# Weight conversion: the sign comes from ScalarE's scaling step instead of a VectorE step

## The chip, the cores and the metric

One core of a Trainium2 chip. The metric is the device time of one execution in microseconds; the kernel before took 1156.26 us (median of 3 runs, 1155.57 to 1157.02).

## The reference

Three stages, computed in float32 on the chip. The weights `moe_*` and `moe2_*` come from numpy as 64-bit floats and are handed over as 64-bit words; q, k, v are 32-bit.

```python
q_n, k_n = rmsnorm(q, g_q), rmsnorm(k, g_k)          # 4 x 12 heads, 448 x 64
attn = softmax(q_n @ k_n.T / sqrt(64))
x = attn @ v                                         # -> 1792 x 768
x = ((x @ w1) * (x @ w2)) @ w3 @ w_out               # d_ff 1024
h = x @ w_in                                         # d_ff 2048
out = (h * clip(h + 3, 0, 6) / 6) @ w_out2
```

## The kernel before, in words

Attention runs over 24 pairs of heads in 192 steps (8 per pair) in a pipeline: in step t two matmuls give 112 x 448 scores (L631, L632), VectorE scales them and takes the maximum (L638, then L645), ScalarE takes the exponential one step later (L650), TensorE transposes (L657), ScalarE and VectorE evict (L666, L676), and the products with v follow (L709, L710). Every step then calls `fill(us, aux)`, which puts other work into the gaps: products of the first MLP (`filler`, so many microseconds of TensorE work per step), preparation of its weights (`prep`), and from the first batch of layer 2 on the conversion of weights for the second MLP (`early`).

The first MLP is reordered: `wprime` first multiplies w3 and w_out (matmuls at L256, from 9 to 197 us), then for each of 4 batches `layer1` (L395, L400) and `layer2` (L89 to L91). After 731 us only the second MLP is left (L1247, L1309), on weights that are 32-bit by then.

A weight tile of 64-bit floats is brought in by a DMA on SP's queue (`fetch`, tag `raw`, a ring of 4 slots of 128 x 384 or 128 x 512 double words; `wr`, 2 slots of 128 x 768, for the last eight tiles). `convert` makes 32-bit floats of it in four instructions. `hi` is the upper word of each number, `lo` the lower one, `top` the upper 16 bits of the lower word. L149 (ScalarE) reads `hi` as a 32-bit float and multiplies it by 2^-112, which moves the exponent to its new bias; L150 (ScalarE) turns `top` into the three low mantissa bits; L152 (VectorE) takes the sign bit out of `hi` and puts it into `lo`; L155 (VectorE) shifts `hi` left by three and joins `lo`. The shift pushes the sign bit of `hi` out at the top, which is why L152 saves it first.

The order around it is set by cost counters. Each `yield` of `convert` names a cost (0.7, 0.9, 0.9). `fill` gives `prep` a budget (`aux`: 3 per step while `wprime` runs, then 4 until 8 weights are used, then 2) and steps it until the budget is used up or until `reach` forbids the next item (tiles wait for buffers that products set free). `early` gets 0.95 per step, at most 1.9 saved up. In the prologue, before the first score, twelve items are run one by one by `unit`, with the loads, the norms and the first q and k written out by hand between them. From this program order the framework's scheduler makes the order on each engine by a simulated timeline; every engine, and SP's queue with the loads, then runs its instructions in that order, and each waits for its data.

Of the kernel before, what the change touches and what calls it, by code (L numbers as in the profile page):

```python
# [14 lines left out]
F32R = mybir.dt.float32r  # L15
I32 = mybir.dt.int32
U16 = mybir.dt.uint16
SIGN = -(1 << 31)
AF = mybir.ActivationFunctionType
ALU = mybir.AluOpType  # L20
AX = mybir.AxisListType
# [30 lines left out]
def fused_kernel(ctx: ExitStack, tc: tile.TileContext, nat, qT, kT, vin, gq, gk,  # L52
                 w12, w3t, wo, win, wo2, outT):
    nc = tc.nc
# [87 lines left out]
    def convert(w, r):  # L142

        hi, lo = r[:, :, 1], r[:, :, 0]
        top = r.bitcast(U16).rearrange("p n (t s) -> p n t s", s=2)[:, :, 0, 1]
        f = hi.bitcast(F32)
        nc.scalar.activation(f, f, AF.Copy, scale=2.0 ** -112)  # L149
        nc.scalar.activation(lo, top, AF.Copy, scale=2.0 ** -13, bias=2.0 ** -14 - 0.5)  # L150
        yield 0.7
        nc.vector.scalar_tensor_tensor(out=lo, in0=hi, scalar=SIGN, in1=lo,  # L152
                                       op0=ALU.bitwise_and, op1=ALU.bitwise_or)
        yield 0.9
        nc.vector.scalar_tensor_tensor(out=w, in0=hi, scalar=3, in1=lo,  # L155
                                       op0=ALU.logical_shift_left, op1=ALU.bitwise_or)
        yield 0.9


    prep = [None]  # L160
# [15 lines left out]
    def open_wprime():  # L176
# [29 lines left out]
        def item(q):  # L206
            kind, n, z = order[q]
            r = raw.pop(q)
            w = r.shape[1]
            if kind != "l":  # L210
                if kind == "c":
                    t = woh[n, z] = pool.tile([P, NH], F32, tag="woh", bufs=2 * M1, name="woh")
                else:
                    t = w3[n, z] = pool.tile([P, HF], F32, tag="w3", bufs=NA3, name="w3")
                if r.dtype == F32:
                    nc.gpsimd.tensor_copy(t, r)
                else:
                    yield from convert(t.bitcast(I32), r)
                load(q + 4)
                return  # L220
            if z == 0:
                W["first"][n] = W["hp"].tile([P, 2, DM], F32R, tag="ws", bufs=NF, name="ws")
            t = W["first"][n][:, :, z * NH : z * NH + NH]
            f = r
            if r.dtype != F32:
                wi = r[:, :, 0]
                yield from convert(wi, r)
                f = wi.bitcast(F32)
            nc.scalar.activation(t[:, 0, :], f, AF.Copy)
            yield w / 1200  # L230
            W["sub"] = nc.gpsimd.tensor_sub(t[:, 1, :], f, t[:, 0, :])
            if z == 1:
                dma(w12d[n // 2, 1 - n % 2], W["first"][n].bitcast(F32).rearrange("p t c -> p (t c)"))
            load(q + 4)
            yield 0.0
# [51 lines left out]
    def early():  # L287
        pool = L["xp"]
        todo = [(x, h) for x in reversed(EARLY) for h in range(2)]
        raws = []  # L290

        def load():
            if todo:
                (kind, q), h = todo.pop()
                cs = slice(h * NH, h * NH + NH)
                src = (win if kind == "in" else wo2)[q][:, cs]
                raws.append((fetch(pool, src, NH, "raw", 4), wfd[q + (M2 if kind == "out" else 0)][:, cs]))

        load()
        yield 0.5  # L300
        while raws:
            r, dst = raws.pop()
            load()
            w = pool.tile([P, NH, 2], I32, tag="raw", bufs=4, name="raw").rearrange("p n t -> p (n t)")[:, :NH]
            yield from convert(w, r)
            dma(dst, w.bitcast(F32))
            yield 0.0
# [133 lines left out]
    state = dict(debt=0.0, aux=0.0, early=0.0, spent=0.0, done=False)  # L441

    def fill(us, aux):

        state["aux"] = min(state["aux"] + aux, 2 * aux)
        while state["aux"] > 0 and prep[0] is not None:
            c = prep[0].step()
            if c is None:
                break
            state["aux"] -= c  # L450
        state["early"] = min(state["early"] + 0.95, 1.9)
        while state["early"] > 0 and "early" in L:
            c = next(L["early"], None)
            if c is None:
                break
            state["early"] -= c
        state["debt"] = min(state["debt"] + us, 2 * us)
        while state["debt"] > 0 and not state["done"]:
            try:
                c = next(filler)  # L460
            except StopIteration:
                state["done"] = True
                return
            if c is None:
                return
            state["debt"] -= c
            if "pool" in L:
                state["spent"] += c
# [5 lines left out]
    def attention(ap, rate):  # L474
# [273 lines left out]
        z = 4 * NC * D  # L748
# [4 lines left out]
            dma(T["nat", i], nat[i].rearrange("p a b d -> p (a b) d"))  # L753

        def unit(q, n):
            for z in range(4):
                prep[0].step()
            assert prep[0].done == q + 1
            load(n)

        load(0)
# [8 lines left out]
        dma(gs[:, 1:2], gk)  # L770
        nc.vector.tensor_mul(G, gs[:, 0:1], gs[:, 1:2])
        unit(0, 4)
        unit(1, 5)
        load_q(0)
        load_k(0)
# [7 lines left out]

        squares(0)
        unit(2, 6)
        squares(1)
        unit(3, 7)
# [36 lines left out]
        unit(11, 15)  # L824
        load_nat(4)
        fill(8.0, 0.0)
        queue[1] = False
        first = ExitStack()
# [51 lines left out]
        while t < 8 * NP + 23 or xs_ready:  # L880
            t += 1
            if t == 4:
                first.close()
            now[0] = t
            live = t < 8 * NP
            ps = score(*divmod(t, 8)) if live else None
            if 0 < t <= 8 * NP:
                expo(*divmod(t - 1, 8))
            u = t - LG
            if 0 <= u < 8 * NP and u % 8 < 7:  # L890
                trans(*divmod(u, 8))
            if 0 <= u - 1 < 8 * NP and (u - 1) % 8 < 7:
                tlo(*divmod(u - 1, 8))
            if live:
                scale_max(t // 8, t % 8, ps)
                negate(*divmod(t, 8))
            if 0 <= u < 8 * NP and u % 8 < 7:
                thi(*divmod(u, 8))
            if 0 <= u - 2 < 8 * NP and (u - 2) % 8 < 7:
                pv(*divmod(u - 2, 8))  # L900
            with ExitStack() as es:
                for a in anchors.get(t - (3 if "pool" in L else 2), ()):
                    es.enter_context(tc.issue_after(a.ins))
                fill(*rate(t))
            run_tasks()
            if "pool" in L:
                xnext()
# [254 lines left out]
    while not state["done"] or any(k >= now[0] for k in tasks):  # L1162
        now[0] += 1
        fill(2.0, 3.0)
        run_tasks()
        if "half" in L and xg is None:
            xo["cm"] = tc.tile_pool(name="xl", bufs=1, side="left", **RW)
            xo["pool", True] = d1.enter_context(xo["cm"])
            xg = xprep(0)
        with ExitStack() as es:  # L1170
            for z in L["gate"].values():
                es.enter_context(tc.issue_after(z.ins))
            if xg is None:
                spend(1.1)
            else:
                for _ in range(2):
                    if next(xg, None) is None:
                        prep_to(ready[0] + 1 if ready[0] < AHEAD2 else 0)
# [245 lines left out]
```

## Time and profile before

| | |
|---|---|
| median of 3 runs | 1156.26 us |
| profiled execution | 1154.9 us, span 1153.1 us |
| PE (matmul) busy | 1109.7 us, 96% |
| PEld (weight load) busy | 944.3 us, 82% |
| DVE (VectorE) busy | 924.0 us, 80%, 2047 instructions |
| ACT (ScalarE) busy | 815.5 us, 71%, 1729 instructions |
| POOL (GpSimd) busy | 185.9 us, 16% |
| DMA | 299.04 MB, 259 GB/s in the mean |

The profile is that of one execution. Busy shares are means over stages with different limits, so the stages have to be read one by one. L with a number is a line of the kernel; "x" a count of instructions; `raw<-raw` names the tile written and the tile read. The chain of waits follows the work that ended last back through whatever released it.

### The profile page before, as it was taken

The numbers are of one execution on the slowest core, as the hardware profiler recorded it, in microseconds if no ns is written. First come the engines' busy times: TensorE is split into PE (matmuls) and PEld (weight loads), VectorE is DVE, ScalarE is ACT, GpSimd is POOL, SyncE is SP. The second block draws the span as 40 slices with busy tenths as digits, with TensorE's granted clock in tenths as the row PEclk, the third lists the DMA queues.
The fourth block names the chain that finished last, engine by engine and source line by source line (L and its number), as shares of the span: only waits on it lengthen the run. The fifth ranks groups of instructions, "written<-read, shape, count | busy, mean of one in ns | idle before, by whom it ended". The sixth has DMA issues, their size and how long they took to land.

```text
span 1153.1 us, 17490 instructions
## 1 busy us (share of the span) xinstructions
PE 1109.7 (96%) x5483; PEld 944.3 (82%) x5483; DVE 924.0 (80%) x2047; ACT 815.5 (71%) x1729; POOL 185.9 (16%) x156
## 2 busy tenths in 40 slices
PE   5899899899999999999999999999999999999998
PEld 3455576788788888788999899899988989999897
DVE  7878988889878998889875345899988898887764
ACT  6888878888678877688675333766666776666664
POOL 1132422645422222223002000000000000000000
PEclk9999999999999999999999999999999999999999
DMA  8988845789999889898879989556469955435961
GB/s 266 332 269 292 268 156 155 232 271 292 329 314 326 287 307 310 275 306 278 274 268 313 393 327 349 218 199 208 163 224 381 368 169 169 154 109 174 343 233 73
DMA packets 109661, 299.04 MB, mean 259 GB/s; under 512 B 13280, under 2 KB 46048, under 8 KB 109568
## 3 DMA queue, kind: packets, MB, share of 16 engines
q1 hardware_dynamic: 109568, 297.93, 75.8%
q8 instruction: 43, 0.70, 0.3%
q14 instruction: 50, 0.41, 0.1%
HBM read 230.61 MB, written 67.27 MB: 258 GB/s over the span
## 4 chain that ended last, share of the span: by engine, by line
PE 59%; DVE 14%; DMA 12%; ACT 9%; issue 3%; SPq 1%; POOL 1%; ACTq 0%; POOLq 0%; DVEq 0%
PE acc L1309 17%; PE sB L1247 8%; PE sA L1247 8%; PE bank L395 6%; PE bank L256 4%; PE bank L400 3%; DVE PP L638 3%; PE bank L657 2%; DMA raw<-in_wo_dram 2%; DMA rsd<-rss 2%; DVE xl L676 2%; DMA rsb<-rsd 2%; DMA raw<-in_w_dram 2%; DVE raw L152 2%; DVE Q L604 2%
## 5 line engine op out<-in xcount | busy, mean ns | idle before, releaser
L1309 PE MATMUL acc<-g,wt 128*128 128x448 f32 x1008 | 214.8, 369 | 1.2 <-ACT g L1197 1.0
L1309 PEld LDWEIGHTS acc<-g,wt 128*128 128x128 f32 x1008 | 189.1, 188 | 20.6 <-ACT g L1197 1.9
L395 PE MATMUL bank<-xhl,ws 128*128 128x448 f32 x768 | 181.0, 367 | 2.8 <-ACT bs L416 1.5
L395 PEld LDWEIGHTS bank<-xhl,ws 128*128 128x128 f32 x768 | 143.6, 188 | 16.3 <-ACT bs L416 1.9
L650 ACT ACTIVATE PP<-PP,mx 112x448 f32<-112x448 f32 x192 | 127.3, 664 | 39.3 <-DVE mx L645 37.1
L638 DVE CUSTOM_DVE_ANT_0 PP<-bank,rb,rq 112x448 f32<-112x448 f32 x192 | 128.4, 673 | 12.3 <-PE bank L632 10.3
L256 PE MATMUL bank<-woh,w 128*128 128x384 f32 x256 | 99.9, 515 | 14.3 <-DVE woh L155 12.4
L1247 PE MATMUL sA<-xo,wt 128*128 128x448 f32 x504 | 112.0, 366 | 1.1 <-ACT u L1258 1.1
L1247 PE MATMUL sB<-xo,wt 128*128 128x448 f32 x504 | 112.2, 367 | 0.8 <-ACT u L1258 0.6
L1247 PEld LDWEIGHTS sB<-xo,wt 128*128 128x128 f32 x504 | 94.4, 188 | 9.9 <-ACT u L1258 1.9
L1247 PEld LDWEIGHTS sA<-xo,wt 128*128 128x128 f32 x504 | 94.6, 188 | 9.5 <-ACT u L1258 1.5
L657 PEld LDWEIGHTS bank<-ident,PP 112*128 112x128 f32 x672 | 77.8, 140 | 29.6 <-issue 8.8
L666 ACT ACTIVATE xh<-bank 128x448 fp32r<-128x448 f32 (+1 forms) x156 | 82.7, 538 | 27.3 <-PE bank L657 22.5
L152 DVE SCALAR_TENSOR_TENSOR raw<-raw 128x384 int32<-128x384 int32 (+1 forms) x112 | 69.3, 619 | 39.8 <-ACT raw L150 35.9
L676 DVE TENSOR_TENSOR xl<-bank,xh 128x448 fp32r<-128x448 f32 x142 | 86.8, 614 | 16.3 <-ACT xh L666 15.1
L657 PE MATMUL bank<-ident,PP 112*128 112x112 f32 x672 | 93.7, 260 | 4.7 <-DVE xl L676 3.0
L1016 DVE TENSOR_TENSOR wt<-wf,wt 128x384 fp32r<-128x384 f32 x160 | 86.8, 552 | 14.0 <-ACT wt L1015 13.8
L400 PE MATMUL bank<-xhl,ws 128*128 128x448 f32 x384 | 94.7, 366 | 0.0
L149 ACT ACTIVATE raw<-raw 128x384 f32<-128x384 f32 (+1 forms) x112 | 63.7, 569 | 41.4 <-DMA raw<-in_wo_dram 16.6
L631 PE MATMUL bank<-K,Q 128*112 128x448 f32 x192 | 79.9, 417 | 6.4 <-DVE mx L638 6.2
L256 PEld LDWEIGHTS bank<-woh,w 128*128 128x128 f32 x256 | 49.4, 199 | 43.8 <-DVE woh L155 15.5
L1015 ACT ACTIVATE wt<-wf 128x384 fp32r<-128x384 f32 x160 | 80.3, 517 | 2.9 <-PE acc L1309 2.7
(136 smaller groups left out, 2181.7 us busy)
## 6 DMA issues: line engine op xcount, KB each, us to landing
ws<-w12d SPq DMA_DIRECT2D x48, 768.0 KB
ws<-wpd SPq DMA_DIRECT2D x32, 768.0 KB
wf<-wfd SPq DMA_DIRECT2D x56, 384.0 KB
raw<-in_wo_dram SPq DMA_DIRECT2D x44, 384.0 KB
td<-G SPq DMA_DIRECT2D x32, 448.0 KB
G<-td SPq DMA_DIRECT2D x32, 448.0 KB
raw<-in_w_dram SPq DMA_DIRECT2D x32, 384.0 KB
w12d<-ws SPq DMA_DIRECT2D x16, 768.0 KB
```

Of the source, the lines that this page charges most:

```text
L152: nc.vector.scalar_tensor_tensor(out=lo, in0=hi, scalar=SIGN, in1=lo, op0=ALU.bitwise_and, op1=ALU.bitwise_or)
L256: nc.tensor.matmul(ps[:, :NH], W["w3"][a, c // 4][:, cs], W["woh"][c, n], start=c == 0, stop=c == M1 - 1)
L395: nc.tensor.matmul(ps[:, :S], w[:, 0, ks], x[:, y, :], start=k == 0 and y == 0, stop=False)
L400: nc.tensor.matmul(ps[:, :S], w[:, 1, ks], L["xhl"][i][:, 0, :], start=False, stop=k == KD - 1)
L638: anchors[8 * i + s].append(nc.vector.tensor_tensor_reduce(out=T["PP", i][:, c, sl], in0=ps[:CP, :S], in1=T["rb", i][:, sl], op0=ALU.mult, ...
L650: anchors[8 * i + s].append(nc.scalar.activation(v, v, AF.Exp, bias=T["m", i][:, 8 + s : 9 + s], accum_out=T["sum", i][:, s : s + 1]))
L657: nc.tensor.transpose(ps[:, c * CP : c * CP + CP], src[:, c, kb * P : kb * P + P], ident[:CP, :CP])
L666: nc.scalar.activation(hi, ps, AF.Copy)
L676: nc.vector.tensor_sub(lo, ps, hi)
L1016: nc.vector.tensor_sub(t[:, 1, :], src, t[:, 0, :])
L1247: mm = nc.tensor.matmul(ps[:, :S], w[:, a, ks], x[:, c, :], start=first and k == 0 and n == 0, stop=k == KD // 2 - 1 and n == 2, skip_grou ...
L1309: nc.tensor.matmul(ps, w[:, y, ns], x[:, z, :], start=first and a == 0, stop=end and a == 2, skip_group_check=h in "674")
```

## The change

ScalarE's scaling becomes a parametric rectifier: a value that is negative after the scale is also multiplied by alpha = 2^32, which adds 32 to its exponent field. Shifted left by three, that added bit lands where the sign of the result is, and the old sign bit falls out as before. So L152's instruction isn't needed, and its `yield` goes with it. The paid cost of `early` per step is cut from 0.95 to 0.6, its cap from 1.9 to 1.2. `unit` runs its item until it is done instead of in four steps.

```diff
-SIGN = -(1 << 31)
...
-        nc.scalar.activation(f, f, AF.Copy, scale=2.0 ** -112)
+        nc.scalar.activation(f, f, AF.Prelu, scale=2.0 ** -112, alpha=2.0 ** 32)
         nc.scalar.activation(lo, top, AF.Copy, scale=2.0 ** -13, bias=2.0 ** -14 - 0.5)
         yield 0.7
-        nc.vector.scalar_tensor_tensor(out=lo, in0=hi, scalar=SIGN, in1=lo,
-                                       op0=ALU.bitwise_and, op1=ALU.bitwise_or)
-        yield 0.9
         nc.vector.scalar_tensor_tensor(out=w, in0=hi, scalar=3, in1=lo,
                                        op0=ALU.logical_shift_left, op1=ALU.bitwise_or)
         yield 0.9
...
-        state["early"] = min(state["early"] + 0.95, 1.9)
+        state["early"] = min(state["early"] + 0.6, 1.2)
...
-            for z in range(4):
+            while prep[0].done <= q:
                 prep[0].step()
-            assert prep[0].done == q + 1
             load(n)
```

## Rows read from the trace of the kernel before

**Rows 1.** Windows: stretch, length, engine busy (instructions), clock, DMA share, GB/s.

```profile
0.00:29.00 29.00, 15.73 (x54) 8.97 (x55) 20.51 (x36) 19.49 (x32) 3.33 (x8) 1.00 0.83 265
29.00:60.00 31.00, 27.76 (x103) 14.90 (x101) 25.18 (x69) 27.41 (x64) 4.81 (x4) 0.94 0.99 331
60.00:100.00 40.00, 39.06 (x146) 21.03 (x146) 28.72 (x72) 32.90 (x75) 12.12 (x10) 1.00 0.86 282
100.00:150.00 50.00, 45.16 (x194) 28.77 (x195) 46.61 (x125) 41.98 (x92) 16.96 (x15) 1.00 0.80 254
150.00:200.00 50.00, 50.00 (x242) 35.28 (x240) 41.37 (x120) 39.77 (x90) 14.03 (x12) 1.00 0.51 159
200.00:306.00 106.00, 98.73 (x520) 83.01 (x519) 98.03 (x230) 91.23 (x205) 53.05 (x44) 1.00 0.83 273
306.00:420.00 114.00, 112.95 (x619) 100.01 (x618) 96.42 (x247) 88.01 (x195) 31.55 (x26) 1.00 0.92 305
420.00:530.00 110.00, 105.33 (x565) 91.62 (x564) 96.48 (x240) 86.46 (x191) 30.21 (x25) 0.98 0.91 303
...
731.00:1153.00 422.00, 415.47 (x2018) 378.09 (x2016) 347.15 (x659) 280.06 (x574) 0.00 (x0) 1.00 0.61 216
sum 1153.00, PE 1109.66 PEld 944.30 DVE 924.00 ACT 815.51 POOL 185.92; mean PE 85.36 PEld 72.64 DVE 71.08 ACT 62.73 POOL 14.30
```

**Rows 2.** Windows of L638 alone: two records for each attention step.

```profile
60.00:100.00 40.00, 7.03 (x21) 1.00 0.86 282
...
150.00:200.00 50.00, 14.18 (x42) 1.00 0.51 159
```

**Rows 3.** Groups by line: conversions; busy us, mean ns, idle before and releaser.

```profile
L152 DVE SCALAR_TENSOR_TENSOR raw<-raw 128x384 int32<-128x384 int32 (+1 forms) x112 | 69.3, 619 | 39.8 <-ACT raw L150 35.9 <-issue 3.5
...
L149 ACT ACTIVATE raw<-raw 128x384 f32<-128x384 f32 (+1 forms) x112 | 63.7, 569 | 41.4 <-DMA raw<-in_wo_dram 16.6 <-DMA raw<-in_w_dram 12.0 <-DMA raw<-in_win_dram 6.5
...
L152 DVE SCALAR_TENSOR_TENSOR wr<-wr 128x768 int32<-128x768 int32 x8 | 7.6, 954 | 15.5 <-ACT wr L150 15.5
```

**Rows 4.** Chain by line, of 0:29, 29:60, 60:100, 100:150 and 200:306 in turn.

```profile
by line: DMA raw<-in_wo_dram 44.1%; DMA nat<-in_nat_dram 22.2%; DVE Q L604 7.6%; DVE raw L152 6.7%; issue 5.2%; ACT raw L149 3.8%; DVE rr L554 3.7%; SPq L100 3.0%; ACT raw L150 2.7%; DVE w L155 2.5%; DVE rt L549 0.7%; DVE rt L551 0.7%; ACT 
...
by line: PE bank L256 31.1%; DMA raw<-in_wo_dram 13.0%; PE bank L705 11.6%; issue 9.0%; PE bank L631 6.8%; PE bank L657 6.7%; DVE PP L638 6.3%; DVE raw L152 5.9%; PE bank L632 4.5%; DVE woh L155 3.5%; PE bank L691 2.9%; DVE Q L604 2.3%; ACT
...
by line: DMA raw<-in_w_dram 25.9%; PE bank L256 18.8%; ACT raw L150 8.4%; DVE raw L152 6.1%; ACT raw L149 5.9%; issue 5.2%; PE bank L705 4.5%; PE bank L657 3.6%; DVE PP L638 3.0%; ACT ws L229 2.8%; DVE raw L155 2.6%; ACT PP L650 2.6%; PE ba
...
by line: DMA raw<-in_w3t_dram 11.0%; issue 10.3%; DMA rsd<-rss 8.3%; DVE PP L638 8.0%; DMA vr<-in_v_dram 6.8%; DVE w L155 5.2%; PE bank L256 5.2%; DVE raw L152 3.9%; DVE xl L676 3.6%; PE bank L657 3.5%; DVE Q L604 2.9%; SPq L100 2.9%; PE ba
...
by line: DVE PP L638 11.9%; DMA raw<-in_w_dram 8.2%; issue 6.6%; DVE Q L604 6.0%; DVE xl L676 5.9%; DMA rsb<-rsd 5.6%; DVE raw L155 4.9%; DVE raw L152 4.7%; ACT PP L650 4.2%; ACT raw L150 3.8%; ACT raw L149 3.6%; DVE ss L522 3.4%; ACT ws L3
```

**Rows 5.** The page's chain by line, share of the whole span.

```profile
PE acc L1309 17%; PE sB L1247 8%; PE sA L1247 8%; PE bank L395 6%; PE bank L256 4%; PE bank L400 3%; DVE PP L638 3%; PE bank L657 2%; DMA raw<-in_wo_dram 2%; DMA rsd<-rss 2%; DVE xl L676 2%; DMA rsb<-rsd 2%; DMA raw<-in_w_dram 2%; DVE raw L152 2%; DVE Q L604 2%
```

**Rows 6.** Timeline: start, length, ACT's longest wait for a raw load here.

```profile
80.95 0.55 ACT L149 ACTIVATE raw<-raw 128x384 f32<-128x384 f32 x1 [4.34 <-DMA raw<-in_w_dram]
```

**Rows 7.** Windows of L152 alone.

```profile
60.00:100.00 40.00, 7.83 (x12) 1.00 0.86 282
...
100.00:150.00 50.00, 6.21 (x9) 1.00 0.80 254
...
200.00:306.00 106.00, 14.14 (x22) 1.00 0.83 273
```

**Rows 8.** Groups by line: ACT's nearest forms, and the table load.

```profile
L1197 ACT ACTIVATE g<-G 128x448 fp32r<-128x448 f32 x80 | 45.9, 580 | 42.7 <-PE acc L1309 41.7 <-ACT wt L1015 0.9
...
L1189 ACT ACTIVATE u<-u,half 128x448 f32<-128x448 f32 x64 | 41.1, 664 | 7.0 <-DVE u L1268 7.0
...
L514 ACT ACTIVATE nat<-nat 112x1024 f32<-112x1024 f32 x20 | 21.0, 1051 | 3.2 <-DMA nat<-in_nat_dram 3.1
...
L610 ACT ACTIVATE K<-kr 128x896 fp32r<-128x896 f32 x24 | 22.6, 941 | 0.0
...
L55 ACT ACT_TABLE_LOAD x1 | 1.3, 1283 | 0.7 <-PEq L1414 0.7
```

## The prediction

> **What bounds the kernel now.** I read the windows by stage first, then the conversion's own groups, then the chain of waits cut into the same stages. The windows [rows 1] show two kernels in one. From 731 us to the end TensorE is busy 415.47 of 422 us; no conversion stands there, so the change cannot reach it. From 306 to 530 us it is also nearly full (112.95 of 114 and 105.33 of 110 us). Before that it has air: it is busy 15.73 of the first 29 us, 45.16 of 50 us from 100 to 150, 98.73 of 106 us from 200 to 306, and the overlapping matmul records flatter it, since its weight loads fill only 21.03 of 40 us from 60 to 100. In these early stages three others are close to full: VectorE (25.18 of 31, 46.61 of 50, 98.03 of 106 us), ScalarE (27.41 of 31, 32.90 of 40, 91.23 of 106) and the DMA engines (share 0.99 from 29 to 60, 0.86 from 60 to 100). The pace of attention shows what this costs: a step leaves two records at L638, so 60 to 100 us holds 10.5 steps of 3.8 us, and 150 to 200 us, where no weight is converted, holds 21 of 2.4 us [rows 2].
>
> The step that goes is L152. It is 112 + 8 instructions, 69.3 + 7.6 = 76.9 us of VectorE's 924.00 [rows 1, 3], 619 ns in the mean. In the chain it has a smaller part: 6.7% of the first 29 us (1.9 us), 5.9% of 29 to 60 (1.8), 6.1% of 60 to 100 (2.4), 3.9% of 100 to 150 (2.0) and 4.7% of 200 to 306 (5.0), together 13.1 us [rows 4]; of the whole span it has 2%, some 23 us [rows 5], so about 10 us lie between 306 and 700. These 23 us are a ceiling: the time that the chain would lose if nothing else came late in L152's place.
>
> **Part 1, the VectorE step goes.** I take from each share what I think isn't handed to the next in line.
> - 0 to 29: 1.9 us on the chain. The same rows give 44.1% and 22.2% to loads, and ScalarE waits for raw data; but near the end of the stretch VectorE works without a gap, and the conversions there stand ahead of the first score. I take 1.0.
> - 29 to 60 and 60 to 100: 1.8 + 2.4. Next in line are the raw loads (13.0% and 25.9% of the chain) [rows 4], and the DMA engines are nearly full. One ScalarE wait for such a load takes 4.34 us, with the exponentials of attention queued behind it [rows 6]. A raw slot comes free some 0.6 us earlier, so its next load is issued earlier, which helps only where the engines have room. I take 0.8 + 1.0.
> - 100 to 150: 2.0 on the chain; VectorE is busy 46.61 of 50 us and loses 6.21 [rows 1, 7]; the DMA share is down to 0.80. I take 1.0.
> - 200 to 306: here VectorE is the fullest engine, and L152 has 14.14 of its 98.03 us [rows 1, 7]. Of the 5.0 on the chain I take 3.0; behind it come ScalarE with 91.23 of 106 us and TensorE, whose idle time is 7.3 us in all.
> - 306 to 700: of some 10 us I take 1.0, since TensorE's idle time is 1.05 us from 306 to 420 and 4.7 from 420 to 530, and after attention it is nearly full.
>
> Sum: 1.0 + 0.8 + 1.0 + 1.0 + 3.0 + 1.0 = 7.8 us. Bounds: nothing (TensorE, ScalarE and DMA hide all of it) to 23 us.
>
> **Part 2, Prelu instead of Copy on ScalarE.** The instruction count on ScalarE stays. The trace has no Prelu, so I bound it by neighbours [rows 8]. From the Copies at 448 and 896 elements (580 and 941 ns) an element costs 0.81 ns, so 1024 elements would take 1044; Square, another function than Copy with immediate operands, takes 1051. That is +7 ns. The upper end is the Relu with a bias tile, 664 against 580 ns for the same shape: +84 ns, by 120 instructions 10 us of ScalarE, of which the chain would get perhaps a tenth to a fifth, as L149 has 3.8 to 5.9% of it where it shows [rows 4], so 1 to 2 us. Below nothing I see no reason: elements and bytes are the same as in the Copy. I take 0, by the row nearest to an immediate-operand form, Square.
>
> The Trainium skill ("ScalarE: Activation LUTs", section What ACT_TABLE_LOAD costs) says that each per-partition pointer operand adds about 93 ns; the trace's 84 agrees. If scale or alpha came as pointers here, by that page it would be 11 us of ScalarE work, the same upper end.
>
> **Part 3, the pace.** The generator of a conversion now hands out 0.7 + 0.9 = 1.6 units of cost and not 2.5. The weights for the early stage of the second layer are paid 0.6 per step and not 0.95: 0.6/1.6 = 0.375 conversions per step against 0.38, so they keep their places. The `Prep` budget stays at 3 per step: 3/1.6 = 1.9 conversions per step against 1.2, wherever free buffers allow it. So from about 29 to 100 us, and in the first batch of layer 1, conversions stand earlier among the attention steps. That helps where the products wait for weights and hurts where a conversion placed early makes ScalarE wait for its load. The scheduler also lays out the whole order anew, which can move single waits either way. For both together I take 0 and keep 14 us upward (the first rival) and 5 us downward (TensorE idles 3.24 + 0.94 + 4.84 us between 29 and 150 [rows 1], about half of which earlier weights could fill). The loop in `unit` makes one step fewer for a conversion, ends at the same place and costs nothing.
>
> **Sum.** The profiled execution took 1154.9 us (span 1153.1 and 1.8 around it); 1154.9 - 7.8 = 1147.1. It lay 1.4 below the median 1156.26, so the forecast is 1148.5 us.
>
> **Rivals.**
> *Earlier conversions choke the loads (slower).* If DMA sets the time from 29 to 100 us (shares 0.99 and 0.86), the conversions of that stretch take its 71 us however they are placed. At 1.9 per step what stood among 20 steps stands among about 14, and 6 steps are pushed into the time after it, at 2.4 us each [rows 2]: +14 us at most, less the DMA work that these steps took along, so 10 or so. The gains up to 150 us (3.8) are lost, the 4.0 from later ones stay: 1156.3 + 10 - 4 = 1162 us. For it: the DMA share and the 4.34 us wait [rows 1, 6]. Against it: the reach of `Prep` (buffers freed by products) holds back part of the items, and the scheduler can place work that is ready ahead of them. It decides from the point where ScalarE's waits for raw loads between 29 and 100 us grow by more than the 3.8 us that are gained.
>
> *TensorE and DMA hide it all (no change).* 1156 us. For it: TensorE is busy 1109.66 of 1153 us [rows 1]. Against it: L152 on the chain in every early stage.
>
> *VectorE was the bound (larger gain).* All of the chain's share comes off: 1156.3 - 23 = 1133 us. For it: 98.03 of 106 us from 200 to 306. Against it: ScalarE is nearly as full, and TensorE idles too little after 306.
>
> *Prelu costs more than Copy.* With +84 ns the sum is 7.8 - 2, so 1150.5 us; for it only the missing row.
>
> *The change doesn't do what it says.* If Prelu were not in the table that is loaded once at the start (L55, 1283 ns [rows 8]), ScalarE would reload tables around conversions, since Exp runs between them: 120 conversions by two loads by 1.28 us, up to 308 us, some 1460 us in all. The Trainium skill (same page, section Table sets: the hidden batching unit) speaks against it for simple functions such as relu and copy, which it says are in every set, but its list names no Prelu; by it a switch costs 2.66 us with the drain. The trace has one load, so no run shows a switch yet.
>
> **How the numbers follow.** Forecast (1143 to 1153) 0.44; larger gain 0.12; dearer Prelu 0.06 (0.05 of it still faster); no change 0.15; choked loads 0.20; table loads and other mishaps 0.03. A measurement of this kernel can tell about 0.2% (2.3 us) from no change. Faster: 0.44 + 0.12 + 0.05 = 0.61; within 0.2%: 0.15 + 0.01 = 0.16; slower: 0.20 + 0.03 = 0.23. The range from 1136 to 1163 leaves out about half of the larger gains, somewhat under half of the choked cases and the table loads.
>
> **What would show it.** In the changed profile: VectorE's busy time near 847 us, no instruction at L152's step, 120 Prelus near 570 ns (the 384 and 512 forms) and one table load. From 200 to 306 us the stage ends some 3 us earlier, and the stretch from 731 to the end is as long as now. Wrong would be: the second MLP starting no earlier; steps from 29 to 100 us longer than now with more ScalarE waits for raw loads; Prelu above 600 ns.

## The result, and the profile after

The changed kernel takes 1144.76 us (median of 4 runs, 1141.81 to 1150.48) against 1156.64 us before: ratio 0.9898, 95% interval 0.9851 to 0.9946. Run again on another chip of the same kind it took 1145.32 against 1154.49 us: 0.9912 (0.9880 to 0.9944). So it is faster by some 1.0%, 9 to 12 us; the forecast was 1148.5 us, 7.8 less.

The windows of the changed kernel, cut as in [rows 1] (PE, PEld, DVE, ACT and POOL busy, then clock, DMA share, GB/s), with its second MLP from 720.9 us on as the last row:

```profile
0.00:29.00 29.00, 15.63 (x57) 9.06 (x57) 16.05 (x31) 19.29 (x32) 3.30 (x8) 1.00 0.84 262
29.00:60.00 31.00, 28.98 (x112) 16.40 (x113) 21.51 (x68) 31.00 (x73) 6.70 (x6) 1.00 1.02 331
60.00:100.00 40.00, 38.51 (x144) 20.70 (x143) 22.69 (x63) 34.41 (x76) 11.92 (x12) 1.00 1.00 332
100.00:150.00 50.00, 47.83 (x217) 32.53 (x216) 43.88 (x117) 42.75 (x97) 14.57 (x13) 1.00 0.75 243
150.00:200.00 50.00, 48.96 (x237) 34.58 (x236) 42.14 (x119) 39.70 (x89) 17.10 (x15) 1.00 0.53 167
200.00:306.00 106.00, 103.75 (x553) 89.39 (x553) 86.86 (x212) 91.11 (x206) 51.51 (x45) 1.00 0.86 298
306.00:420.00 114.00, 111.19 (x604) 98.92 (x603) 85.82 (x235) 89.25 (x200) 27.57 (x23) 0.99 0.89 295
420.00:530.00 110.00, 107.05 (x583) 93.81 (x583) 90.59 (x237) 87.14 (x195) 29.26 (x24) 1.00 0.90 301
720.90:1140.00 419.10, 412.42 (x2018) 377.95 (x2017) 347.09 (x659) 279.46 (x574) 0.00 (x0) 1.00 0.62 218
```

What to see here is that VectorE drops out of the first place. From 60 to 100 us it is busy 22.69 of 40 us (28.72 before), from 200 to 306 us 86.86 of 106 (98.03 before), while TensorE's instructions in that stretch rise from 520 to 553. Beside TensorE, whose matmul records overlap, ScalarE is now the fullest: all of 29 to 60 us and 34.41 of 40 from 60 to 100, with the DMA engines at 1.02 and 1.00.

The page's busy rows, and the groups by line (busy us, mean ns, idle before) that answer to [rows 3] and to the table load of [rows 8]:

```profile
PE 1103.1 (97%) x5483; PEld 944.0 (83%) x5483; DVE 850.8 (75%) x1927; ACT 812.4 (71%) x1729; POOL 177.9 (16%) x156
```

```profile
L148 ACT ACTIVATE raw<-raw 128x384 f32<-128x384 f32 (+1 forms) x112 | 63.8, 569 | 28.6 <-DMA raw<-in_wo_dram 11.6 <-DMA raw<-in_w_dram 6.5 <-DMA raw<-in_w3t_dram 5.4
...
L149 ACT ACTIVATE raw<-raw 128x384 int32<-128x384 uint16 (+1 forms) x112 | 63.2, 565 | 0.0
...
L151 DVE SCALAR_TENSOR_TENSOR raw<-raw 128x384 int32<-128x384 int32 x80 | 48.9, 613 | 46.0 <-ACT raw L149 38.8 <-issue 6.1 <-POOL K L608 0.6
...
L54 ACT ACT_TABLE_LOAD x1 | 1.3, 1283 | 0.7 <-PEq L1409 0.7
```

The line numbers have shifted: L148 is the Prelu (L149 before), L149 is ScalarE's second step (L150 before), L151 is the one VectorE step left (L155 before). The Prelu takes 569 ns, to the nanosecond the Copy's mean. L151 waits for ScalarE's second step, 38.8 us in the row; that wait isn't new, it stood at L152 with 35.9 us [rows 3]. One table load, as before.

Where the time came from is read best from the start of every score record (L638 before, L634 after) in the two timelines. Step 0 is the first; the lead is how much earlier the changed kernel gets there. The last three columns are the leads of runs told below. Each column rests on one profiled execution, so a lead of 1 or 2 us can be that execution's or that chip's: two runs told below that leave the first stage as it was stand 1.8 and 2.1 us behind at step 64.

| step | before, us | after, us | lead | L152 twice | layer 1 and second MLP alone | without ScalarE's second step |
|---|---|---|---|---|---|---|
| 0 | 28.2 | 26.2 | 2.0 | -2.9 | -0.5 | 1.9 |
| 16 | 69.6 | 58.0 | 11.5 | 2.1 | -1.3 | 10.0 |
| 24 | 102.0 | 96.2 | 5.7 | -0.3 | -0.5 | 10.6 |
| 32 | 121.2 | 117.7 | 3.4 | -12.2 | -0.5 | 7.3 |
| 64 | 200.1 | 193.5 | 6.6 | -16.1 | -0.9 | 11.0 |
| 96 | 313.6 | 299.6 | 14.0 | -17.6 | 9.4 | 22.1 |
| 128 | 407.9 | 399.1 | 8.8 | -27.1 | 0.6 | 23.6 |
| 191 | 586.3 | 573.3 | 12.9 | -31.6 | -0.8 | 25.4 |

The lead is won early, shrinks from 11.5 to 3.4 us between steps 16 and 32, and comes back. How steady this is can be seen in two more profiles, of the changed kernel run again and of Prelu at the old pace, both told below: at step 64 the leads of the three are 6.6, 6.9 and 6.3 us, at step 96 14.0, 15.2 and 11.1, and at the start of the second MLP 10.0 (730.9 to 720.9), 6.4 and 13.3. So what is won up to step 64 repeats, and what comes after scatters by several us.

The rest of the 13.1 us between the two spans lies in the second MLP, where nothing was changed. That stretch took 422.2 us before and 419.1 after:

```profile
730.90:1153.10 422.20, 415.57 (x2018) 378.18 (x2017) 347.25 (x659) 280.06 (x574) 0.00 (x0) 1.00 0.61 216
```

It took between 418.2 and 422.7 us in the other kernels of this study that do the same work there in the same number of matmuls: 422.2 with Prelu in the first stage only, and 420.4 with L152 kept and the pace alone changed. So I don't count those 3 us as the change's; this is argued from the spread, not shown.

### The profile page after: what moved, and what is told of

Its sections match the earlier page's. It is cut to its first block, busy times and chain, and to the rows that moved or that the text cites. A ratio compares the mean times of both kernels' runs of the same rounds, so it can differ in the third digit from the quotient of the medians.

```text
span 1140.0 us, 17361 instructions
## 1 busy us (share of the span) xinstructions
PE 1103.1 (97%) x5483; PEld 944.0 (83%) x5483; DVE 850.8 (75%) x1927; ACT 812.4 (71%) x1729; POOL 177.9 (16%) x156
## 4 chain that ended last, share of the span: by engine, by line
PE 60%; ACT 7%; DMA 7%; DVE 3%; issue 2%; POOL 0%; SPq 0%; ACTq 0%; POOLq 0%; DVEq 0%
PE acc L1304 17%; PE bank L391 10%; PE sB L1242 8%; PE sA L1242 8%; PE bank L396 5%; DMA rsb<-rsd 2%; PE bank L653 2%; ACT PP L646 1%; PE bank L88 1%; PE bank L89 1%; PE bank L90 1%; PE bank L627 1%; PE bank L628 1%; PE bank L706 1%; DMA raw<-in_wo_dram 1%
## 5 line engine op out<-in xcount | busy, mean ns | idle before, releaser
L1304 PE MATMUL acc<-g,wt 128*128 128x448 f32 x1008 | 211.7, 366 | 1.2 <-ACT g L1192 1.0
L634 DVE CUSTOM_DVE_ANT_0 PP<-bank,rb,rq 112x448 f32<-112x448 f32 x192 | 128.7, 675 | 27.4 <-PE bank L628 21.1
L252 PE MATMUL bank<-woh,w 128*128 128x384 f32 x256 | 97.6, 509 | 14.6 <-DVE woh L151 10.9
L672 DVE TENSOR_TENSOR xl<-bank,xh 128x448 fp32r<-128x448 f32 x142 | 87.4, 617 | 11.5 <-ACT xh L662 10.1
L148 ACT ACTIVATE raw<-raw 128x384 f32<-128x384 f32 (+1 forms) x112 | 63.8, 569 | 28.6 <-DMA raw<-in_wo_dram 11.6
L151 DVE SCALAR_TENSOR_TENSOR raw<-raw 128x384 int32<-128x384 int32 x80 | 48.9, 613 | 46.0 <-ACT raw L149 38.8
```

The costliest lines, as they stand in the source:

```text
L252: nc.tensor.matmul(ps[:, :NH], W["w3"][a, c // 4][:, cs], W["woh"][c, n], start=c == 0, stop=c == M1 - 1)
L634: anchors[8 * i + s].append(nc.vector.tensor_tensor_reduce(out=T["PP", i][:, c, sl], in0=ps[:CP, :S], in1=T["rb", i][:, sl], op0=ALU.mult, ...
L672: nc.vector.tensor_sub(lo, ps, hi)
L1304: nc.tensor.matmul(ps, w[:, y, ns], x[:, z, :], start=first and a == 0, stop=end and a == 2, skip_group_check=h in "674")
```

## The experiments

Twelve runs, each timed against the kernel before in several rounds. Ratios are to the kernel before on the same chip. The first four were timed on one chip (kernel before 1154.49 us), the parts alone and the moved loads on a second (1156.66), the pairs and the last run on a third (1154.08).

**The changed kernel again.** No edit.

> The changed kernel once more, unaltered, as the measure of the others on this chip. Theory A (VectorE's work ahead of attention's steps was late, its removal gives the gain), theory B (the gain comes from the conversions being placed earlier by the smaller costs) and theory C (any new order moves the time by some us, whatever is changed) all expect some 0.990 of the kernel before, 1145 us; C allows other values.

Measured: 1145.32 us, 0.9912 (0.9880 to 0.9944). It is the measure for the others.

**Prelu at the old pace.** The placement of the conversions is kept as before.

```diff
         yield 0.7
+        yield 0.9
         nc.vector.scalar_tensor_tensor(out=w, in0=hi, scalar=3, in1=lo,
                                        op0=ALU.logical_shift_left, op1=ALU.bitwise_or)
...
-        state["early"] = min(state["early"] + 0.6, 1.2)
+        state["early"] = min(state["early"] + 0.95, 1.9)
```

> L152 is gone and Prelu is in, but a conversion costs 2.5 as before (a yield of 0.9 kept where L152 stood) and early is paid 0.95 as before. Theory A: the gain stays, 0.990, 1145 us (1141 to 1150). Theory B: the gain goes, 0.999, 1155 us. Theory C: anything from 1140 to 1160.

Measured: 1145.98 us, 0.9905 (0.9869 to 0.9941). The gain stays whole; its lead of 11.6 us at step 16 and 3.1 at step 32 repeats the changed kernel's. So the new pace isn't needed for the gain, nor for the loss between these steps.

**The pace alone.** L152 kept, its cost gone; the loop in `unit` is the changed kernel's.

```diff
         nc.vector.scalar_tensor_tensor(out=lo, in0=hi, scalar=SIGN, in1=lo,
                                        op0=ALU.bitwise_and, op1=ALU.bitwise_or)
-        yield 0.9
...
-        state["early"] = min(state["early"] + 0.95, 1.9)
+        state["early"] = min(state["early"] + 0.6, 1.2)
```

> The kernel before with L152 kept, but a conversion costs 1.6 (no cost for L152) and early is paid 0.6: the pace alone. Theory A with pace at nothing: 1.000, 1156 us. Theory B: 0.990, 1145 us. The choked-loads rival of the prediction: 1160 to 1165 us, as nothing is gained on VectorE in exchange. Theory C: anything from 1150 to 1165.

Measured: 1152.84 us, 0.9991 (0.9964 to 1.0017). Theory B and the choked loads fall together: with these costs the conversions do no harm and no good that can be told from noise.

**L152 twice.**

```diff
         nc.vector.scalar_tensor_tensor(out=lo, in0=hi, scalar=SIGN, in1=lo,
                                        op0=ALU.bitwise_and, op1=ALU.bitwise_or)
+        nc.vector.scalar_tensor_tensor(out=lo, in0=hi, scalar=SIGN, in1=lo,
+                                       op0=ALU.bitwise_and, op1=ALU.bitwise_or)
```

> The kernel before with L152 issued twice in each conversion (the second repeats the first), costs as before: 77 us more on VectorE. Theory A: VectorE is near its limit in the early stages, so it costs at least what the removal gives, 8 to 25 us: 1164 to 1181 us. If TensorE and DMA hid VectorE (the no-change rival): 1156 to 1158 us. Theory C: within 5 us of 1156.

Measured: 1184.63 us, 1.0276 (1.0234 to 1.0318), slower by 31.9 us at the ratio. That is above the range given. Windows of this kernel, columns as above:

```profile
60.00:100.00 40.00, 37.32 (x143) 19.07 (x142) 34.52 (x79) 30.32 (x69) 9.07 (x7) 1.00 0.81 255
100.00:150.00 50.00, 43.62 (x166) 26.95 (x164) 48.62 (x110) 38.30 (x81) 16.64 (x13) 0.93 0.82 268
200.00:306.00 106.00, 97.28 (x482) 77.30 (x481) 101.16 (x235) 85.00 (x192) 49.81 (x39) 0.97 0.67 216
306.00:420.00 114.00, 110.09 (x596) 95.86 (x595) 103.84 (x257) 87.15 (x193) 37.00 (x29) 1.00 0.94 317
```

VectorE is busy 48.62 of 50 and 101.16 of 106 us. TensorE and ScalarE fall back in all four stretches against [rows 1], the DMA share only from 60 to 100 and from 200 to 306 us (0.67 instead of 0.83). A further 77 us on VectorE cost 32 us, 0.41 us for each; the 77 us taken away gave 9 to 12 us, 0.12 to 0.16 for each. So the kernel before stood at a knee: VectorE's work costs more going up than it gives going down. The second L152 fills VectorE and also makes the way from load to weight longer by one instruction, as the removal makes it shorter; no run takes the two apart.

**One part at a time.** A flag sends only some callers of `convert` through the new branch; costs as before.

```diff
-    def convert(w, r):
+    def convert(w, r, new=False):
...
-        nc.scalar.activation(f, f, AF.Copy, scale=2.0 ** -112)
+        if new:
+            nc.scalar.activation(f, f, AF.Prelu, scale=2.0 ** -112, alpha=2.0 ** 32)
+        else:
+            nc.scalar.activation(f, f, AF.Copy, scale=2.0 ** -112)
```

First stage only:

> Prelu without L152 only in the 42 conversions of the first stage (prologue and wprime), costs as before. Theory A1 (each stage gives its own part, and it stays): the prediction's terms up to 150 us are 3.8 us, the changed kernel's step 64 came 6.6 us earlier: 1148 to 1151 us, 0.995. Rival A2 (what the first stage gains is taken back later): 1154 to 1156 us.

Measured: 1151.67 us, 0.9942 (0.9916 to 0.9967). Its profiled execution, 1154.41 us, was the longest of twelve (1144.19 at the shortest), so its leads, 3.3 us at step 64 and 0.7 at step 191, say little.

Layer 1 only:

> Prelu without L152 only in the 22 conversions of layer 1's first batch, costs as before. Theory A1: the prediction's term is 3.0 us, between steps 64 and 128 the changed kernel gained a further 2.2 us (7.4 at step 96): 1149 to 1152 us, 0.996. Rival A2: TensorE is the next limit there and what is won is lost by step 128: 1154 to 1156 us.

Measured: 1157.57 us, 1.0005 (0.9974 to 1.0035).

The second MLP's conversions only:

> Prelu without L152 only in the 56 conversions for the second MLP, costs as before. Theory A1: the prediction's term is 1.0 us; the changed kernel gained 4.1 us from step 128 to step 191: 1150 to 1153 us, 0.997. The prediction's view that TensorE is full there: 1153 to 1155 us.

Measured: 1158.21 us, 1.0013 (0.9993 to 1.0033).

The first stage alone gives more than half. The two others alone give no gain in the time: of A1 only the first stage's part holds. The score records say more of layer 1. Alone, it goes from 1.8 us behind the kernel before at step 64 to 8.5 us ahead at step 96: the stage itself wins some 10 us, where the changed kernel won 7.4 (6.6 to 14.0). At step 128 1.5 us are left, and at step 191 it is 5.6 us behind. That is its rival A2, what is won is lost by step 128. What takes it back is open. For the second MLP's conversions the view that TensorE is full there fits. The three sum to -0.40%, and all together give -0.9%. So pairs were run:

> Prelu without L152 in the first stage and in layer 1, not in the second MLP's conversions; costs as before. Alone these parts gave 0.9942 and 1.0005. Theory A3 (the parts only pay together: a later stage uses its freer VectorE only when it is also relieved elsewhere): 0.991 to 0.993, 1147 us, if layer 1 is the partner of the first stage. Theory A4 (parts add): 0.9947, 1150.5 us.

Measured: 1143.96 us, 0.9920 (0.9890 to 0.9951).

> Prelu without L152 in the first stage and in the second MLP's conversions, not in layer 1; costs as before. Theory A3: 0.991 to 0.993, 1147 us, if the second MLP's conversions are the partner of the first stage. Theory A4: 0.9955, 1151.5 us.

Measured: 1143.71 us, 0.9923 (0.9892 to 0.9953).

> Prelu without L152 in layer 1 and in the second MLP's conversions, not in the first stage; costs as before. Theory A4 (parts add): 1.002, 1158 us. Theory A3: if the two only pay together, 0.995 to 0.997, 1152 us.

Measured: 1149.36 us, 0.9967 (0.9945 to 0.9988).

Each pair lies below the sum of its parts (0.9947, 0.9955 and 1.0018): the first sum is inside the pair's interval, the second on its edge, the third outside. But a sum of two parts is itself uncertain by 0.3 to 0.4% each way, and the parts were timed on another chip than the pairs, so only the third comes near to speaking for A3. Its profile doesn't bear it out: the lead is 9.4 us at step 96, gone at step 191 and 0.6 us at the start of the second MLP. Nearly all of the 4.5 us by which its span is shorter lies after that, where nothing is converted:

```profile
730.30:1148.60 418.30, 411.54 (x2018) 377.99 (x2017) 347.07 (x659) 279.49 (x574) 0.00 (x0) 1.00 0.61 218
```

So neither A3 nor A4 is shown. What is shown is that the first stage carries most of the gain: alone 0.6%, with either partner 0.8%, with both 0.9 to 1.0%.

**Loads moved out of the crowded stretch.** The changed kernel, with one line of the preparation's order changed.

```diff
-        for a, h in halves:
-            order += [("a", a, h)] + ones[:1]
-            del ones[:1]
-        order += ones
+        order += [("a", a, h) for a, h in halves] + ones
```

> The changed kernel, with the first-layer weights that are prepared ahead (10 half tiles with 5 stores, some 7.5 MB) moved behind all halves of w3 in the order of preparation. Theory D (loads take part of the gain back: the changed kernel is 11.5 us ahead at step 16 and 3.4 at step 32, with a DMA share of 1.00 from 29 to 100 us): the 7.5 MB are some 23 us of DMA at 332 GB/s, moved to a stretch with a share of 0.53 to 0.75, so 3 to 8 us are kept: 1137 to 1142 us, 0.986. Rival (what is lost there is lost to ScalarE or to the order, not to DMA): 1145 us or more, since layer 1 gets its first weights later.

Measured: 1151.35 us, 0.9972 (0.9945 to 0.9999), worse than the changed kernel's 0.9912 on the other chip. Windows:

```profile
60.00:100.00 40.00, 40.00 (x152) 21.66 (x151) 25.78 (x68) 30.12 (x65) 6.69 (x6) 1.00 0.88 290
100.00:150.00 50.00, 46.02 (x204) 31.34 (x203) 40.23 (x111) 43.71 (x99) 19.67 (x18) 0.97 0.77 260
```

From 60 to 100 us the DMA share did fall from 1.00 to 0.88, and the lead was 19.2 us at step 20 and 10.0 instead of 5.7 at step 24. But at step 32 it was 3.1, against 3.4: the same loss came later. It ends in a stretch, 92 to 118 us, where the DMA share is 0.55, ScalarE is busy 19.94 of 26 us and TensorE all 26.00. So theory D falls as put; what takes the lead back in this order, TensorE or the order itself, is not shown.

**Without ScalarE's second step.**

```diff
-        nc.scalar.activation(lo, top, AF.Copy, scale=2.0 ** -13, bias=2.0 ** -14 - 0.5)
         yield 0.7
-        nc.vector.scalar_tensor_tensor(out=w, in0=hi, scalar=3, in1=lo,
-                                       op0=ALU.logical_shift_left, op1=ALU.bitwise_or)
+        nc.vector.scalar_tensor_tensor(out=w, in0=hi, scalar=3, in1=hi,
+                                       op0=ALU.logical_shift_left, op1=ALU.bypass)
```

> The changed kernel without ScalarE's second step of a conversion (the three low mantissa bits are left out; VectorE's remaining step keeps its shape and does not join them): 120 instructions, some 70 us less on ScalarE. Theory E (after the change ScalarE is the next limit while weights are converted, at 34.4 of 40 us from 60 to 100 against VectorE's 22.7): as much again as the change gave, 0.980 to 0.985, 1135 us. Rival (DMA, with a share of 1.00 there, and TensorE are the next limits): 0.988 to 0.992, 1145 us.

Measured: 1130.98 us, 0.9813 (0.9779 to 0.9846): as much again as the change gave. Windows of it:

```profile
60.00:100.00 40.00, 39.80 (x155) 22.28 (x154) 31.52 (x71) 30.16 (x67) 15.65 (x14) 1.00 1.03 348
100.00:150.00 50.00, 48.50 (x218) 32.47 (x217) 42.25 (x119) 40.68 (x91) 14.28 (x13) 1.00 0.76 237
200.00:306.00 106.00, 104.02 (x563) 89.72 (x561) 94.46 (x213) 84.61 (x187) 50.92 (x45) 1.00 0.89 294
```

The same loads run at a DMA share of 1.03 from 60 to 100 us, and most of the lead that the changed kernel loses there stays (10.0 us at step 16, 10.6 at step 24, 7.3 at step 32). VectorE isn't relieved with it: its step takes 727 ns in the mean instead of 648, and its busy time is 864.1 us instead of 850.8. In the changed kernel ScalarE is busy 13.74 of 14 us from 82 to 96 us and 21.51 of 22 from 96 to 118. So in that stretch ScalarE's part of a conversion is the next limit, more than DMA. The step is also a link between load and weight, 565 ns in the changed kernel; whether it is ScalarE's fullness or that link that counts, this run does not tell apart. Most of what this run wins over the changed kernel comes later: by the table 4.4 us of it stand at step 64 and 14.8 at step 128, where both profiles are of short executions (1125.32 and 1141.81 us).

## Why the prediction was right, point by point

*VectorE's step was late in the early stages.* Right, and shown: the removal gives its gain at either pace, the pace alone gives none, the first stage alone gives more than half, and a second L152 costs 32 us. Whether a fuller VectorE or a longer way from load to weight made it late is not separated. The chain of waits had pointed at it with 2% of the span [rows 5], VectorE's busy share of 80% over the whole span had not.

*Prelu costs nothing over Copy.* Right: 569 against 569 ns in the 112 small tiles, 903 against 901 in the eight large ones (the row before: L149 `wr` at 901 ns). Square had been the right neighbour, Relu with a bias tile the wrong one [rows 8]. One table load stands in the profile, so no reload came with the Prelu. The Trainium skill ("ScalarE: Activation LUTs", section Table sets: the hidden batching unit) says that cheap functions, relu and copy among them, are in every set; it lists no Prelu, and the one load here shows that Prelu needed no switch either.

*The pace is worth nothing.* Right in the sum, by two runs. The rival of the choked loads expected 1162 us and is refuted by the pace alone at 0.9991. The prediction named the point that decides it, ScalarE's waits for raw loads from 29 to 100 us growing by more than 3.8 us: they shrank, from 9.1 to 4.9 us. Its picture had some truth in it: a lead is lost between steps 16 and 32 while the DMA share is about 1.00. But that loss is there at the old pace too, and the run without ScalarE's second step puts most of it on ScalarE's part of the conversion.

*The sum of 7.8 us.* The mechanism held, and 9 to 12 us is near the sum; but the sizes of the terms were off, and some of the nearness is luck, since the errors go both ways. Up to 150 us 3.8 us were taken, and 6.3 to 6.9 were won in the three profiles (the leads at step 64). Of these the terms from 29 to 100 us fell short most: 1.8 us were taken, while the lead grew by 3.7 us from step 0 to step 24. There I gave most of L152's share away to DMA, but its share of 0.86 from 60 to 100 us left room [rows 1], and it ran at 1.00 after. From 200 to 306 us 3.0 were taken, and from step 64 to step 96 the lead grew by 7.4 us (8.3 and 4.8 in the two other profiles). In two of the three that is more than the 5.0 us that L152 has on the chain there, so a stage's share of the chain was no ceiling for the stage. After 306 us 1.0 more was taken; from step 96 to the start of the second MLP the lead shrank by 4.0 us in this profile and by 8.8 in the second, and grew by 2.2 in the third. So that term isn't confirmed, not even in its sign.

*The ceiling of 23 us.* The 23 us come from a page that gives whole per cents. Added up piece by piece, L152 has 18.4 us of the chain before, 13.2 up to 306 us and 5.2 behind it, where the prediction put some 10. The ceiling was not reached, so the larger-gain rival, which wanted all of it, is out. What would come late next was named as loads, ScalarE and TensorE; for steps 16 to 32 the runs put ScalarE's second step ahead of the loads. The no-change rival ended with twice L152, which would have cost next to nothing if TensorE and DMA hid VectorE's time.

*The signs.* VectorE's busy time is 850.8 us (847 forecast). The second MLP was to take as long as before: its 3.1 us less in the profile go against the letter of it, but the same work took 418.2 to 422.7 us whatever was edited.

## What to carry to other kernels

Where several engines are nearly full in a stage, an instruction's part in that stage's chain of waits was here a nearer measure of its removal than its busy time (18.4 us on the chain, 77 us busy, 9 to 12 us gained), and it was still too high, since the next engine in line takes the rest: look for it in the same window before pricing. Doubling the suspected step is a cheap test of which side of the knee a kernel stands on. A lead won in one stage has to be followed to the end of the kernel: layer 1 alone won 10 us and kept none. A follow-up should go to the step that leads after the change, here ScalarE's second conversion step.

## What the runs showed that I had not expected

Work was worth some three times as much added as removed: 0.41 us per us of VectorE against 0.12 to 0.16. And relief in layer 1 alone gave 10 us in its own stage and nothing in the time (1.0005). Whether parts of the change pay more together than alone is suggested by one pair (0.9967 against 1.0018) and not shown.
